# A two-branch sequence kernel: a new written order with finer steps, exchanges issued by SyncE, shared slots and a lead-in of unread products

## The chip, the core and the metric

The kernel runs on one core of a Trainium2 chip. The core has five engines, each with its own queue of instructions that it works through in order: TensorE (PE; its weight loads are listed apart as PEld), VectorE (DVE), ScalarE (ACT), GpSimd (POOL) and SyncE (SP). SP here only issues DMAs, POOL issues DMAs and does a little set-up. Engines wait for each other through semaphores. The metric is the device time of one launch in microseconds; lower is better.

## What is computed

The reference concatenates two results along the last axis, each of 2,048 steps (S) by 1,024 channels (D):

```
A: k_shift = sum over t of k shifted by t steps, times shift_k[:, t]   (4 taps)
   kv = k_shift * v
   y  = irfft(rfft(kv, 2S) * rfft(ssm_k, 2S))[:S] + kv * ssm_D          (long convolution)
   out_a = q * y
B: Lam_bar = exp(dt * Lam), B_bar = ((Lam_bar - 1) / Lam) * B           (complex, 1,024 states)
   h[t] = Lam_bar * h[t-1] + B_bar x[t]
   out_b = 2 * Re(C h) + x * Dskip
```

## The kernel before

**Branch B** takes the sequence in 16 chunks of 128 steps. For chunk i, `x` (L439) loads x transposed. `U` (L444) multiplies it by B on TensorE, into a PSUM bank for every two of the eight groups of 128 states (four calls per chunk, 32 products of 128 columns each); `ue` (L455) copies the bank to SBUF on ScalarE. VectorE then turns the complex recurrence into a real one by a rotation: `r1` (product with the table Z1), `r2` (sum, and from the second chunk the carry), `sc` (two scans of 1,024 elements, and two small instructions that make the next carry), `r3` (product with Z2), `r4` (sum). `y` (L499) multiplies by C on TensorE, `ye` copies, `yst` stores. B and C reach their layout by loads (`bl`, `cl`), transposes on TensorE (`bT`, `cT`) and copies (`bc`, `cc`); eight pieces of C come by transposing DMAs instead (`cx`, L435).

**Branch A** does the convolution as a transform over 4,096 points in two stages, 256 by 16. Stage one: `kvm` and `kva` (L540, L551) make the shifted and weighted k times v on VectorE, `am` multiplies by the constants F1, `ae` copies, `ast` stores to the DRAM tensor Ys_kv. The filter goes the same way: `hl` loads ssm_k, `hT` transposes it, `hc` copies, `hm` multiplies, `he` copies, `hst` stores to Ys_h. Stage two has 32 groups. `lh` and `lk` (L632) load two groups of each tensor at a time in another layout, `lw` (L627) loads the constants W of two groups. For group g: `sh` and `sk` multiply on TensorE (L641), `she` and `ske` copy to SBUF on ScalarE (L651, L660). `sw` (L663) makes a second copy of the filter's result with its upper and lower 64 partitions exchanged, by two DMAs of 128 KB within SBUF. `pr` (L671) multiplies both copies with the other result on VectorE, `sa` (L680) does the inverse stage on TensorE, `sae` copies, `vst` (L693) stores to Vs. Last, `vl` loads Vs in a third layout, `a3` multiplies by G, `a3e` copies, `qm` multiplies by q (loaded by `qp`), `ost` stores.

**What sets the order.** Nothing is scheduled at run time. The string ORDER lists some 1,560 words, such as `U.0.0:p1a6`: the step, its indices, and after the colon the slots of its new tiles. The last loop of the kernel calls the steps in that order, and every engine's queue gets its instructions in the order in which they are called. Two words on different engines are ordered only by the data and by the slots that they share. Slots p0 to p7 are the PSUM banks; b0 to b14 are SBUF tiles of 2 KB per partition; a0 to a10 are tiles of 4 KB (loads of v, q, ssm_k, Vs, and the tiles u, h, hab, vsb); m0 and m1 are VectorE's products; w0 to w2 the constants W. The loads `lh` and `lk` have six slots of their own, h0 to h2 and k0 to k2, in a pool (a2) that takes the place of the one that holds wbc and the ring of k when stage one is done. A new tile in a slot waits until the last reader of the old one is done. DMAs called `spd` (loads, and the transposing ones) go into SP's queue, those called `gpd` (stores, the exchanges, a few constants) into POOL's.

Of the kernel before, what the change touches and what calls it, by code (L numbers as in the profile page):

```python
# [14 lines left out]
ALU = mybir.AluOpType  # L15
F32 = mybir.dt.float32
BF16 = mybir.dt.bfloat16
# [45 lines left out]
CFG = {'kr': 8, 'bdve': 4, 'actsw': ()}  # L63

ORDER = """
ld_par ld_w:a0a1 ld_G bl.2.0:b0 ld_sd bl.0.1:b1 bl.2.1:b2 ld_F x.0:b3 wb.4:p0 bl.3.0:b4 wb.0:p1 bl.7.1:b5 wbe.4 par_T:p2 bl.5.0:b6 wbe.0 bl.5.1:b7
bT.2.0:p3 p32 bl.4.1:b8 exp1 wb.1:p4 bl.0.0:b9 bc.2.0 dve2 bT.0.1:p5 bl.1.0:b10 dve3 wbe.1 sm_pre wb.2:p6 exp2 wb.3:p7 bl.4.0:b11 wbe.2 bT.2.1:p0 dd
wbe.3 cx.7.0 sin0 bT.3.0:p1 bT.7.1:p2 bc.3.0 bl.1.1:b12 wb.5:p3 bl.7.0:b13 bc.0.1 bT.5.0:p4 wbe.5 wb.6:p6 bl.3.1:b14 bc.2.1 bT.5.1:p7 bc.7.1 wb.7:p1
tabA1:a2a3a4a5 cx.6.0 bT.4.1:p5 bc.5.1 bT.0.0:p3 cx.7.1 wbe.6 bT.1.0:p0 bc.4.1 bT.4.0:p2 kp.-2 wbe.7 par_rest bc.0.0 bl.6.0:b0 bc.5.0 x.2:b1 bT.1.1:p7
bc.1.0 bT.7.0:p6 bc.1.1 x.1:b2 tabA2 bT.3.1:p5 bc.7.0 U.0.0:p1a6 hl.0.0:a7 bc.4.0 cl.2.1:b4 bc.3.1 sin2 U.0.1:p3 bl.6.1:b5 ue.0.0 sin1 kp.-1 U.0.2:p4  # L70
ue.0.1 kp.0 eo cl.1.0:b6 bT.6.0:p7 U.2.0:p0a8 hl.0.1:a9 U.1.0:p6a10 cl.2.0:b7 vp.0:a0 ue.2.0 stt U.1.1:p2 cl.1.1:b8 ue.0.2 ue.1.0 bc.6.0 x.3:b9
cT.2.1:p5 ue.1.1 U.1.2:p1 cc.2.1 kp.1 vp.1:a1 z1 cl.0.0:b10 cT.1.0:p3 kvm.0:m0 bT.6.1:p0 U.2.1:p4 cl.3.0:b11 cl.3.1:b12 cc.1.0 kvm.1:m1 U.2.2:p6 z2
kp.2 bc.6.1 cx.4.1 kva.0:b13 cT.1.1:p7 hT.0.0:p2 ue.1.2 vp.2:a2 U.0.3:p5 cc.1.1 ue.2.1 kva.1:b14 cx.5.1 hc.0.0:b0 am.0.0:p3 am.0.1:p0 am.0.2:p1 ue.0.3
am.0.3:p7 U.1.3:p4 cl.0.1:b4 ue.2.2 ae.0.0:b6 cx.4.0 r1.0:m0 ae.0.1 ae.0.2:b5 am.1.0:p2 am.1.1:p5 ast.0.0 ae.0.3 hl.1.0:a3 am.1.2:p6 am.1.3:p3
ae.1.0:b8 cx.5.0 cT.3.0:p0 ast.0.1 ae.1.2:b13 U.2.3:p1 kvm.2:m1 cc.3.0 hl.2.0:a4 ae.1.3 cT.0.0:p7 ae.1.1 ast.1.1 cT.3.1:p2 lw.0:w0 ue.2.3 r2.0:a5
hT.0.1:p6 ast.1.0 cc.0.0 cT.2.0:p0 kva.2:b14 hT.0.2:p3 cc.3.1 hT.0.3:p5 cc.2.0 U.3.0:p1a0 hl.1.1:a6 hc.0.1:b11 sc.0 hc.0.3:b10 am.2.0:p7 am.2.1:p2
am.2.2:p0 am.2.3:p6 ae.2.0:b12 cx.6.1 hm.0.3.0:p5 ae.2.1 hm.0.3.1:p7 ae.2.2:b7 hm.0.3.2:p2 ast.2.0 ae.2.3 x.4:b6 cT.0.1:p0 he.0.3.2:b5 U.3.1:p6
ast.2.1 cc.0.1 he.0.3.0:b14 kvm.3:m0 kp.3 he.0.3.1 U.3.2:p2 ue.3.1 hst.0.3.0 ue.3.0 hc.0.2:b13 r3.0:m1 U.3.3:p0 x.6:b4 ue.3.2 ue.1.3 hm.0.2.0:p5
ue.3.3 hm.0.2.1:p7 hd.0 hm.0.1.0:p6 r4.0 hm.0.3.3:p1 he.0.2.0:b8 hm.0.0.0:p3 x.5:b12 hm.0.0.1:p2 he.0.1.0:b10 hm.0.2.2:p4 hm.0.2.3:p0 he.0.0.0:b7
hm.0.1.1:p5 r1.1:m1 y.0.0.0:p6 he.0.0.1 he.0.1.1 y.0.0.1 hst.0.0.0 he.0.3.3 he.0.2.1 x.7:b13 y.0.0.2 he.0.2.2:b14 r2.1:a7 hst.0.3.1 he.0.2.3 y.0.0.3  # L80
hl.2.1:a9 lw.2:w1 hm.0.0.2:p3 sc.1 hm.0.0.3:p2 hst.0.2.1 hT.1.0:p5 ye.0.0:b0 hT.1.1:p1 lw.1:w2 hm.0.1.2:p7 y.0.1.0:p4 hst.0.2.0 y.0.1.1 hst.0.1.0
he.0.0.2:b7 y.0.1.2 x.9:b3 he.0.0.3 y.0.1.3 r1.2:m1 hm.0.1.3:p0 ye.0.1 hT.1.2:p6 hst.0.0.1 hc.1.0:b11 hT.1.3:p3 U.4.0:p2a10 vp.7:a5 hc.1.3:b5 hd.1
r2.2:a3 yst.0 hc.1.2:b14 hm.1.0.0:p4 hm.1.0.1:p5 sc.2 ue.4.0 vp.3:a6 hm.1.0.2:p3 hm.1.0.3:p6 U.4.1:p2 he.0.1.2:b11 he.0.1.3 he.1.0.0:b8 hst.0.1.1
he.1.0.1 U.4.2:p7 ue.4.1 hst.1.0.0 hc.1.1:b10 U.4.3:p0 ue.4.2 r3.1:m1 he.1.0.2:b7 hm.1.1.0:p4 hm.1.1.1:p5 ue.4.3 hm.1.1.2:p2 hm.1.1.3:p1 he.1.0.3
hm.1.3.0:p7 r4.1 hm.1.3.1:p3 hm.1.3.2:p0 he.1.1.2:b10 hT.2.0:p6 hst.1.0.1 he.1.1.3 hm.1.3.3:p2 kva.3:b0 he.1.1.0:b5 y.1.0.0:p1 he.1.1.1 hst.1.1.1
y.1.0.1 y.1.0.2 he.1.3.2:b11 r3.2:m1 hst.1.1.0 vp.6:a8 he.1.3.3 y.1.0.3 y.1.1.0:p4 hst.1.3.1 ye.1.0:b8 r1.3:m0 y.1.1.1 am.3.0:p5 hc.2.0:b2 am.3.1:p0
am.3.2:p2 am.3.3:p1 r4.2 y.1.1.2 x.8:b0 ae.3.2:b7 ae.3.3 y.1.1.3 r2.3:a1 hl.3.0:a0 ast.3.1 y.2.0.0:p6 ye.1.1 ae.3.0:b10 hd.2 sc.3 y.2.0.1 yst.1 ae.3.1
hm.2.0.0:p2 ast.3.0 hm.2.0.1:p1 hm.2.0.2:p4 hm.2.0.3:p5 y.2.0.2 he.2.0.0:b2 he.2.0.1 y.2.0.3 he.2.0.2:b5 hst.2.0.0 he.2.0.3 y.2.1.0:p0 ye.2.0:b11
y.2.1.1 hst.2.0.1 kvm.4:m1 y.2.1.2 he.1.3.0:b1 he.1.3.1 y.2.1.3 x.10:b7 r3.3:m0 hst.1.3.0 hm.1.2.0:p2 ye.2.1 hm.1.2.1:p1 hm.1.2.2:p4 kp.4 hm.1.2.3:p5
he.1.2.0:b8 hT.2.1:p6 he.1.2.2:b14 yst.2 hT.2.2:p7 he.1.2.3 hT.2.3:p3 kva.4:b10 hc.2.2:b2 hst.1.2.1 U.5.0:p0a7 hl.3.1:a3 hc.2.1:b5 he.1.2.1 r4.3  # L90
U.5.1:p2 ue.5.0 hst.1.2.0 kvm.5:m1 hc.2.3:b1 am.4.0:p4 am.4.1:p5 am.4.2:p7 am.4.3:p6 ue.5.1 y.3.0.0:p1 ae.4.2:b10 kvm.6:m0 ae.4.3 y.3.0.1 ae.4.0:b11
ast.4.1 ae.4.1 y.3.0.2 ast.4.0 y.3.0.3 kp.5 kva.5:b14 y.3.1.0:p0 ye.3.0:b8 y.3.1.1 kva.6:b10 y.3.1.2 vp.4:a4 x.12:b9 am.5.0:p3 am.5.1:p2 am.5.2:p7
ae.5.0:b11 am.5.3:p6 y.3.1.3 ae.5.2:b14 kvm.7:m1 ae.5.3 am.6.0:p4 am.6.1:p5 ye.3.1 am.6.2:p1 am.6.3:p3 ast.5.1 ae.5.1 U.5.2:p7 yst.3 ae.6.0:b10 ae.6.1
ast.5.0 r1.4:m0 ast.6.0 hm.2.1.0:p6 ue.5.2 hm.2.1.1:p0 hm.2.1.2:p2 hm.2.1.3:p4 U.5.3:p5 he.2.1.2:b5 r2.4:a9 he.2.1.3 vp.5:a2 he.2.1.0:b14 hst.2.1.1
he.2.1.1 hm.2.2.0:p7 kva.7:b8 hm.2.2.1:p2 ue.5.3 hm.2.2.2:p4 hm.2.2.3:p6 he.2.2.0:b11 hm.2.3.0:p0 hm.2.3.1:p5 hst.2.1.0 he.2.2.1 hm.2.3.2:p7
he.2.3.0:b2 hm.2.3.3:p2 he.2.3.1 hT.3.0:p0 sc.4 hst.2.2.0 he.2.3.2:b10 am.7.0:p5 he.2.3.3 am.7.1:p7 ae.7.0:b1 am.7.2:p2 hst.2.3.1 ae.7.1 am.7.3:p5
he.2.2.2:b5 hT.3.1:p7 he.2.2.3 hT.3.2:p4 ast.7.0 hc.3.1:b8 U.6.0:p6a1 hst.2.3.0 hc.3.2:b14 kvm.8:m0 ae.6.2:b11 hst.2.2.1 hm.3.2.0:p7 hm.3.2.1:p4
ue.6.0 hm.3.2.2:p1 ae.6.3 hm.3.2.3:p6 he.3.2.2:b10 U.6.1:p3 ast.6.1 he.3.2.3 r3.4:m1 kp.6 he.3.2.0:b14 hst.3.2.1 he.3.2.1 ae.7.2:b1 U.6.2:p1 ae.7.3
hst.3.2.0 ue.6.1 kva.8:b2 hc.3.0:b5 hm.3.1.0:p6 hm.3.1.1:p7 hm.3.1.2:p4 ast.7.1 ue.6.2 hm.3.1.3:p2 hT.3.3:p5 he.3.1.0:b8 U.6.3:p3 he.3.1.1 r4.4
hc.3.3:b11 hst.3.1.0 kvm.9:m0 he.3.1.2:b10 y.4.0.0:p0 he.3.1.3 ue.6.3 am.8.0:p1 hst.3.1.1 am.8.1:p6 ae.8.0:b14 am.8.2:p7 am.8.3:p5 kvm.10:m1 y.4.0.1  # L100
ae.8.1 ae.8.2:b1 ast.8.0 y.4.0.2 ae.8.3 y.4.0.3 ast.8.1 kva.9:b2 kp.7 y.4.1.0:p4 ye.4.0:b8 y.4.1.1 kva.10:b10 am.9.0:p2 x.11:b14 am.9.1:p3 ae.9.0:b6
am.9.2:p1 am.9.3:p6 y.4.1.2 ae.9.1 ae.9.2:b2 y.4.1.3 ast.9.0 ae.9.3 kvm.11:m0 hm.3.3.0:p7 ast.9.1 ye.4.1 am.10.0:p5 am.10.1:p0 am.10.2:p2 ae.10.0:b1
hm.3.3.1:p3 yst.4 hm.3.3.2:p1 ae.10.1 am.10.3:p6 hm.3.3.3:p4 ae.10.2:b10 U.9.0:p5a10 kvm.12:m1 ast.10.0 ae.10.3 he.3.3.2:b11 ast.10.1 he.3.3.3
U.9.1:p0 he.3.3.0:b6 hd.3 hst.3.3.1 ue.9.0 kva.11:b2 he.3.3.1 hm.3.0.0:p2 hst.3.3.0 ue.9.1 hm.3.0.1:p6 hm.3.0.2:p1 hm.3.0.3:p4 he.3.0.0:b8 U.7.0:p7a6
he.3.0.1 kva.12:b1 he.3.0.2:b5 hst.3.0.0 he.3.0.3 am.11.0:p5 ue.7.0 am.11.1:p3 am.11.2:p0 am.11.3:p2 ae.11.0:b10 hst.3.0.1 U.7.1:p6 kvm.13:m0 ae.11.1
ae.11.2:b11 ae.11.3 ast.11.0 U.7.2:p1 ue.7.1 ast.11.1 kvm.14:m1 U.7.3:p4 ue.7.2 kva.13:b2 am.12.0:p7 ue.7.3 am.12.1:p5 am.12.2:p3 am.12.3:p0
ae.12.0:b6 U.8.0:p2a0 ae.12.1 kva.14:b8 ae.12.2:b5 ast.12.0 ae.12.3 am.13.0:p6 ue.8.0 am.13.1:p1 ast.12.1 am.13.2:p4 am.13.3:p7 ae.13.0:b10 U.9.2:p5
r1.5:m0 ae.13.1 ae.13.2:b11 ast.13.0 ae.13.3 am.14.0:p3 ue.9.2 am.14.1:p0 ast.13.1 am.14.2:p2 am.14.3:p6 ae.14.0:b1 kvm.15:m1 U.8.1:p1 ae.14.2:b2
ae.14.1 ae.14.3 ast.14.0 U.8.2:p4 ue.8.1 r2.5:a3 ast.14.1 lh.0:h0 lh.1:h1 lh.2:h2 kva.15:b6 U.8.3:p7 ue.8.2 U.9.3:p5 ue.8.3 sc.5 am.15.0:p3 ue.9.3
am.15.1:p2 am.15.2:p0 sh.0.0:p6 ae.15.0:b8 sh.0.1:p1 sh.1.0:p4 ae.15.1 am.15.3:p7 sh.1.1:p5 ae.15.2:b5 U.11.0:p3a4 lh.4:h0 ast.15.0 ae.15.3 she.0.0:a9  # L110
ast.15.1 she.0.1 r1.6:m0 sh.2.0:p2 she.1.0:a2 sh.2.1:p0 sw.0 sh.4.0:p7 she.1.1 sh.4.1:p6 sh.5.0:p1 she.4.0:a8 sh.5.1:p4 sh.3.0:p5 she.5.0:a7 lh.3:h2
# [55 lines left out]
def full_kernel(ctx, tc, A_q, A_k, A_v, A_shift_k, A_ssm_k, A_ssm_D, B_x, B_Lre, B_Lim, B_Bre, B_Bim,  # L167
# [85 lines left out]
    def k4(name, shape):  # L253
        return rtile(ring, "a", name, shape)
# [115 lines left out]
    def z2():  # L370
        nc.scalar.mul(Z2[:, 2, :, :], Z2[:, 0, :, :], -1.0)
        for n_ in ("vc", "vs", "rn", "ang"):
            st.pop(n_)
# [419 lines left out]
```

## Time and profile before

| what | value |
|---|---|
| runs | 389.32, 392.50, 394.33 us; median 392.5 |
| profiled execution | span 394.4 us from its first to its last instruction; the runs list 394.33 |
| TensorE busy | 366.3 us, 93% of the span |
| VectorE busy | 331.7 us, 84% |
| ScalarE busy | 280.4 us, 71% |
| GpSimd busy, with its DMA issues | 126.9 us, 32% |
| DMA | 101.38 MB, 257 GB/s on average |
| first and last product | 5.14 us; the last ends at 388.9 us |
| mean granted TensorE clock | 0.991 |

Times count from the first instruction of the span. A matmul's listed duration runs until its result has left the array, so that two in a row overlap: 128x512 matmuls are listed with 379 ns but start 216 ns apart. "Idle before" is the time in which an engine had nothing before an instruction, and the name behind the arrow is what ended it. In the chain of waits, each line is a piece of the chain that ended last: its start, its length, and who worked; "issue" is time in which nothing is seen to be waited for. In the list of waits, the numbers are the total in us, how often, and the longest. A granted clock of 0.50 means that TensorE ran at half speed.

### The profile page before, as it was taken

What the parts mean: (1) busy time and instruction counts of PE and PEld (TensorE: products, weight loads), DVE (VectorE), ACT (ScalarE), POOL (GpSimd) and SP (SyncE); (2) the same over time, 40 slices, a digit from 0 to 9 for tenths busy, and PEclk for the clock granted to TensorE, in tenths of its full rate; (3) what the DMA queues carried; (4) which work ended last, traced back from release to release, by engine and by line L of the source; (5) the groups of instructions that cost most, each with busy time, mean ns of one, the idle gap of its engine ahead of it and who ended that gap; (6) DMA issues with size and microseconds to landing.
All of it is one profiled execution on the core that took longest, in us unless ns stands there. A gap on an engine that the chain in (4) does not pass through costs nothing.

```text
span 394.4 us, 8923 instructions
## 1 busy us (share of the span) xinstructions
PE 366.3 (93%) x3529; PEld 246.4 (62%) x3529; DVE 331.7 (84%) x335; ACT 280.4 (71%) x519; POOL 126.9 (32%) x220
## 2 busy tenths in 40 slices
PE   4998998999988999999899699899998989999994
PEld 2898886775737858897366244455546458685441
DVE  4766999899989999999999979889956971999941
ACT  4899997676649969769289559589693994344642
POOL 3000124574716765425213233233240341020142
PEclk9999999999999999999999989999998999999999
DMA  6999999999986767368999997999989868458895
GB/s 192 313 250 290 328 234 280 297 239 373 303 199 225 220 190 249 125 199 295 270 269 296 276 239 244 236 330 268 321 244 284 253 161 295 161 181 285 292 359 216
DMA packets 59076, 101.38 MB, mean 257 GB/s; under 512 B 31102, under 2 KB 33150, under 8 KB 59036
## 3 DMA queue, kind: packets, MB, share of 16 engines
q1 hardware_dynamic: 45308, 58.73, 54.5%
q0 software_dynamic: 13728, 42.10, 33.1%
q8 instruction: 27, 0.44, 0.5%
q14 instruction: 13, 0.11, 0.1%
HBM read 52.57 MB, written 33.55 MB: 218 GB/s over the span
## 4 chain that ended last, share of the span: by engine, by line
PE 23%; issue 19%; DMA 12%; POOL 5%; ACT 3%; DVE 3%; POOLq 0%; SPq 0%; ACTq 0%; DVEq 0%
PE ps_y L506 7%; PE ps_a L641 5%; PE ps_a L680 5%; PE ps_u L453 5%; DMA l2k<-Ys_kv 4%; DMA l2h<-Ys_h 3%; DMA wts<-a_c_W 2%; POOL out_dram L726 2%; DMA hab<-hab 2%; ACT hab L651 1%; POOL Ys_kv L576 1%; DMA Ys_kv<-ysb 1%; DVE mt L546 1%; ACT x L660 1%; PE ps_a L565 0%
## 5 line engine op out<-in xcount | busy, mean ns | idle before, releaser
L506 PE MATMUL ps_y<-CT,h 128*128 128x512 bf16 x512 | 127.2, 381 | 1.3 <-DVE h L495 1.3
L453 PEld LDWEIGHTS <-BT 128*128 128x128 bf16 x2048 | 118.6, 99 | 6.1 <-issue 1.8
L453 PE MATMUL ps_u<-xT,BT 128*128 128x128 bf16 x2048 | 122.0, 220 | 0.4
L506 PEld LDWEIGHTS <-h 128*128 128x128 bf16 x512 | 46.0, 98 | 49.9 <-DVE h L495 2.2
L483 DVE TENSOR_TENSOR_SCAN h<-rtab,h 128x1024 bf16<-128x1024 f32 x32 | 71.5, 2274 | 0.2
L455 ACT CAST u<-ps_u 128x512 bf16<-128x512 f32 x64 | 39.9, 645 | 23.1 <-PE ps_u L453 21.5
L624 POOL DMA_DIRECT2D Ys_h<-ysbh x64 | 46.1, 723 | 23.4 <-ACT ysbh L617 20.6
L671 DVE TENSOR_TENSOR hab<-x,hab 128x2048 bf16<-128x2048 bf16 x32 | 38.8, 1222 | 17.4 <-DMA hab<-hab 11.0
L576 POOL DMA_DIRECT2D Ys_kv<-ysb x32 | 17.5, 549 | 87.2 <-ACT ysb L574 87.0
L465 DVE TENSOR_TENSOR mt<-u,Z 128x4096 bf16<-128x4096 bf16 x16 | 36.6, 2286 | 10.5 <-ACT u L455 10.2
L689 ACT CAST vsb<-ps_a 128x512 bf16<-128x512 f32 x64 | 36.0, 638 | 7.8 <-PE ps_a L680 7.8
L660 ACT CAST x<-ps_a 128x512 bf16<-128x512 f32 x64 | 36.9, 665 | 5.9 <-PE ps_a L641 5.8
L651 ACT CAST hab<-ps_a 128x512 bf16<-128x512 f32 x64 | 35.9, 679 | 7.1 <-PE ps_a L641 7.1
L617 ACT CAST ysbh<-ps_a 128x512 bf16<-128x512 f32 x64 | 34.6, 633 | 8.9 <-DMA Ys_h<-ysbh 5.2
L574 ACT CAST ysb<-ps_a 128x512 bf16<-128x512 f32 x64 | 34.3, 634 | 8.8 <-DMA Ys_kv<-ysb 6.1
L521 ACT CAST yo<-ps_y 128x512 bf16<-128x512 f32 x32 | 19.2, 611 | 26.9 <-PE ps_y L506 25.2
L465 DVE TENSOR_TENSOR mt<-h,Z 128x4096 bf16<-128x4096 bf16 x16 | 36.5, 2284 | 0.0
L680 PE MATMUL ps_a<-hab,wts 128*128 128x512 bf16 x128 | 32.4, 379 | 3.8 <-DVE hab L671 3.5
L546 DVE TENSOR_TENSOR mt<-kring,wbc 128x4096 bf16<-128x4096 bf16 (+3 forms) x16 | 29.9, 1884 | 3.4 <-DMA kring<-in_A_k_dram 3.4
L665 POOL DMA_DIRECT2D hab<-hab x32 | 16.8, 526 | 47.1 <-ACT hab L651 45.0
L511 PE MATMUL ps_y<-Dd,xT 128*128 128x128 bf16 x128 | 28.0, 219 | 0.0
L641 PEld LDWEIGHTS <-wts 128*128 128x128 bf16 x128 | 12.1, 99 | 21.0 <-DMA wts<-a_c_W 3.9
(110 smaller groups left out, 448.0 us busy)
## 6 DMA issues: line engine op xcount, KB each, us to landing
Ys_kv<-ysb POOLq DMA_DIRECT2D x32, 256.0 KB, 3.8
Ys_h<-ysbh POOLq DMA_DIRECT2D x64, 128.0 KB, 4.3
l2h<-Ys_h SPq DMA_DIRECT2D x16, 512.0 KB, 6.7
hab<-hab POOLq DMA_DIRECT2D x64, 128.0 KB, 6.7
l2k<-Ys_kv SPq DMA_DIRECT2D x16, 512.0 KB, 6.6
Vs<-vsb POOLq DMA_DIRECT2D x16, 512.0 KB, 4.9
vv<-Vs SPq DMA_DIRECT2D x32, 256.0 KB, 4.2
hk<-in_A_ssm_k_dram SPq DMA_DIRECT2D x8, 512.0 KB, 8.7
```

What stands on the lines that cost most here:

```text
L453: nc.tensor.matmul(pu[:, w, jl, :], BT[:, 2 * jp + jl, w, d, :], xT[:, d, :], start=(d == 0), stop=(d == ND - 1))
L455: E["ue"] = lambda i, jp: nc.scalar.copy(st["u", i][:, :, 2 * jp:2 * jp + 2, :], st.pop(("pu", i, jp))[:])
L465: nc.vector.tensor_mul(m, s_, win(Z))
L483: nc.vector.tensor_tensor_scan(gf[:, a * W:(a + 1) * W], rt1, gf[:, a * W:(a + 1) * W], 0.0, ALU.mult, ALU.add)
L506: nc.tensor.matmul(py[:], h[:, 1 - w, j, :], CT[:, j, w, dh * 512:(dh + 1) * 512], start=(j == 0 and w == 0), stop=(j == NJ - 1 and w == 1))
L617: nc.scalar.copy(st["yh", qd, n4, w // 2][:, :, w % 2, :], st.pop(("pa", qd, n4, w))[:].rearrange("p (c d) -> p c d", c=2))
L624: gpd(Ys_h[cc, n0:n0 + 2, :, qd * DQ:(qd + 1) * DQ].rearrange("n k d -> k n d"), t_[:, cc, :, :])
L651: nc.scalar.copy(st["hab", g][:, 0, cols], pt[:])
L660: nc.scalar.copy(st["x16", g][:, w * 512:(w + 1) * 512], st.pop(("ps", "l2k", g, w))[:])
L671: nc.vector.tensor_mul(hab[:], st.pop(("x16", g))[:].unsqueeze(1).to_broadcast([P, 2, D]), hab[:])
L680: nc.tensor.matmul(pt[:], st["w", gq][:, gi, 1 + a, :], hab[:, a, w * 512:(w + 1) * 512], start=(a == 0), stop=(a == 1))
L689: nc.scalar.copy(st["vsb", gq][:, gi, w * 512:(w + 1) * 512], st.pop(("ps", "v", g, w))[:])
```

## The change

- `fill.10` stands first in the order: ten products of 512 columns of a tile of zeros into a PSUM bank that nobody reads. The zeros are part of Z1, cleared by VectorE at the very start; Z1 gets its values later.
- Steps are cut finer: `U` by one group of states (128 calls of 16 products), `sc` by one scan, with `rc`, `cm` and `ca` for the three carry instructions, `kva` into `kva`, `kvb`, `kvc`. The instructions stay the same; they can be placed one by one.
- `sw` issues its two DMAs from SP's queue instead of POOL's.
- The slots h0 to h2 and k0 to k2 go, and a11 to a16 come, of the same size and in the same pool: `lh` and `lk` draw on all 17 "a" slots, and so do the other users of them late in the kernel.
- The whole order and all slots are new, 1,723 words. Beside the fill, each step occurs as often as before. Tiles are no longer removed from the table `st` when last read, which changes no instruction; an unused option (`actsw`) goes.

What the order changes where the prediction looks: the first loads on SP are `bl.1.0 bl.2.1 bl.3.1`, then the parameters, six more of `bl`, `cl.2.1` and then `x.0`, with `U.0.1.0` as the first U (in the order before: parameters, `bl.2.0 bl.0.1 bl.2.1 x.0`, with `U.0.0` after thirteen transposed tiles of B). The first `cx` comes after all of B. The first `kvm` is `kvm.3`, ahead of `stt` and `r1.0`. `lk.2` is the first load of Ys_kv.

```diff
-CFG = {'kr': 8, 'bdve': 4, 'actsw': ()}
+CFG = {'kr': 8, 'bdve': 4}
+NA = 11
...
-ld_par ld_w:a0a1 ld_G bl.2.0:b0 ld_sd bl.0.1:b1 bl.2.1:b2 ld_F x.0:b3 wb.4:p0 bl.3.0:b4 wb.0:p1 bl.7.1:b5 wbe.4 par_T:p2 bl.5.0:b6 wbe.0 bl.5.1:b7
...
+fill.10:p7 ld_w:a0a1 wb.1:p0 wbe.1 bl.1.0:b0 bl.2.1:b1 bT.2.1:p1 bl.3.1:b2 ld_par ld_F par_T:p2 p32 bl.0.1:b3 exp1 wb.7:p3 wbe.7 bc.2.1 dve2 wb.4:p4 wb.3:p5
...
+sw.7 pr.7 sk.9.1:p2 sk.9.0:p6 y.6.1.1 sw.6 pr.6 ske.9.0:b5 ske.9.1 y.6.1.2 sa.7.0:p2 y.6.1.3 sa.6.0:p6 sae.6.0:a10 sae.7.0 sw.8 pr.8 sa.6.1:p0 sw.9
...
+    Z1 = wpool.tile([P, 3, NJ, T], BF16, name="Z1")
+    nc.vector.memset(Z1[:, 0, 0:4, :], 0.0)
...
     def k4(name, shape):
-        return rtile(ring, "a", name, shape)
+        if cur["a"][0] < NA:
+            return rtile(ring, "a", name, shape)
+        return rtile(ap_pool("a2"), "a", name, shape)
...
+    def fill(n):
+        pt = ptile("ps_z", [P, 512])
+        z = Z1[:, 0, 0:4, :].rearrange("p j t -> p (j t)")
+        for _ in range(n):
+            nc.tensor.matmul(pt[:], z[:, 0:P], z, start=True, stop=True)
...
-    def U(i, jp):
-        if jp == 0:
+    def U(i, jp, jl):
+        if (jp, jl) == (0, 0):
             st["u", i] = k4("u", [P, 2, NJ, T])
...
     def r2(i):
...
-        if i > 0:
-            nc.vector.tensor_add(g[:, :, :, 0], g[:, :, :, 0], carry[:])
...
+    def rc(i):
+        nc.vector.tensor_add(g[:, :, :, 0], g[:, :, :, 0], carry[:])
...
+    def sc(i, a):
+        gf = st["g", i][:].rearrange("p a j t -> p (a j t)")[:, a * W:(a + 1) * W]
+        nc.vector.tensor_tensor_scan(gf, rt1, gf, 0.0, ALU.mult, ALU.add)
...
     def l2(nm, Ys, gq):
-        st[nm, gq] = rtile(ap_pool("a2"), nm[2], nm, [P, GC, D])
+        st[nm, gq] = k4(nm, [P, GC, D])
...
     def sw(g):
         hab = st["hab", g]
-        gpd(hab[0:64, 1, :], hab[64:128, 0, :])
-        gpd(hab[64:128, 1, :], hab[0:64, 0, :])
+        spd(hab[0:64, 1, :], hab[64:128, 0, :])
+        spd(hab[64:128, 1, :], hab[0:64, 0, :])
```

## The prediction

> **What bounds the kernel now.** I read the page first, then busy time by stage, TensorE's timeline at both ends, the chain of waits, the list of waits and the DMA issues.
>
> ```profile
> span 394.4 us, 8923 instructions
> PE 366.3 (93%) x3529; PEld 246.4 (62%) x3529; DVE 331.7 (84%) x335; ACT 280.4 (71%) x519; POOL 126.9 (32%) x220
> ...
> DMA  6999999999986767368999997999989868458895
> ```
>
> TensorE (PE) is nearly always busy, VectorE (DVE) is second, the DMA engines are full until about 120 us. GpSimd (POOL) is idle two thirds of the time. Busy is not full speed, so I price the products by their spacing, from the chain of waits (start, duration, what):
>
> ```profile
> 155.66 0.87 PE ps_a L609 x8
> ...
> 241.57 0.86 PE ps_a L680 x4
> ...
> 257.17 1.79 PE ps_u L453 x32
> ...
> 287.07 0.63 ACT hab L651
> 287.70 0.28 issue
> 287.98 0.48 POOL hab L665
> 288.51 7.61 DMA hab<-hab
> 296.25 1.24 DVE hab L671
> 297.53 1.04 PE ps_a L680 x4
> ```
>
> That is 0.109, 0.216 and 0.056 us for products of 256, 512 and 128 columns. The program has 128, 904 and 2,497 of them (par_T's small one counted with the last): 14.0 + 195.3 + 139.8 = 349.0 us. The span is 394.4, so 45.4 us are not products: 5.1 before the first product starts, 5.4 after the last ends (388.9), and 34.9 lost in between. Spacing the products of each stage in the same way, the loss falls thus: 7.1 in the first 20 us, 7.3 from 20 to 120, 7.0 from 120 to 200, 13.4 from 200 to 340, none after 340.
>
> ```profile
> 0.00:20.00 20.00, 14.86 (x116) 10.67 (x117) 12.53 (x53) 13.75 (x20) 3.66 (x12) 1.00 0.94 250
> 20.00:40.00 20.00, 18.80 (x334) 18.46 (x332) 13.17 (x24) 20.00 (x37) 0.00 (x0) 1.00 1.07 275
> ...
> 227.00:230.00 3.00, 3.00 (x8) 1.08 (x9) 0.50 (x1) 2.15 (x4) 0.20 (x1) 0.50 0.73 90
> ...
> 340.00:360.00 20.00, 20.00 (x196) 13.23 (x194) 19.83 (x18) 7.72 (x15) 2.71 (x5) 1.00 0.63 201
> ```
>
> Columns: stretch, length, busy time of PE, weight loads, DVE, ACT, POOL, granted clock, DMA share, GB/s. Two things to see. DVE has 25.7 us of work in the first 40, so it starts 14.3 us in arrears and is full afterwards. At 227 the granted clock is 0.50, just after a wait of 2.3 us for l2h; it lasts 3.4 us, comes again at 298.7, and costs 1.6 us each time. The start is as slow, though its clock column says 1.00:
>
> ```profile
> 9.54 2.74 PE L417 MATMUL ps_t<-ident,ld 128*128 128x128 bf16 x24
> ```
>
> 24 products in 2.74 us are 0.11 each, half speed. So it goes from 5.1 to about 18.7 us, 4.3 of the 7.1 us lost there; the other 2.8 are gaps.
>
> ```profile
> DVE hab L671 <- DMA hab<-hab: 11.0, 8, 4.6
> ...
> PEld L641 <- DMA wts<-a_c_W: 3.9, 3, 1.7
> ```
>
> ```profile
> l2h<-Ys_h SPq DMA_DIRECT2D x16, 512.0 KB, 6.7
> hab<-hab POOLq DMA_DIRECT2D x64, 128.0 KB, 6.7
> ```
>
> From 180 to 330 us the loop is: TensorE product (sh), ScalarE copy (she), exchange of the halves of hab by two DMAs (sw), VectorE product (pr), TensorE product (sa). The chain above shows one turn: 9.8 us from the end of the copy to sa.
>
> **How I compare the orders.** I add up each queue's work along the two written orders, with these spacings and the groups' mean durations (DVE's scaled to its 331.7 us). A place in TensorE's queue is so many us of products before it; a cover is the products that lie between a cause and its use. These are sums of rows, not a run of the schedule.
>
> **The change part by part.**
> *Fill.* Ten products of 512 columns at half speed, 0.41 us each (four in 1.87 us at 226.96, less the last one's 0.63), are 4.1 us. They need a small memset on VectorE first (today's of ones ends at 0.99 us), so they run from about 1.2 to 5.3; the first real product starts at 5.14 now. Own cost 0.2. If the clock is then full, 4.3 us of half speed go. But loads then bind: x.0 is now the eleventh large DMA on SP's queue (3.5 us issue today, about 7 then, landing near 13 at the 250 to 300 GB/s of this stage), and U starts at queue place 6.3 instead of 8.1, at 20.3 us today. 13 − 6.3 leaves TensorE 6.7 us late where it is 12.2 late today. ScalarE, saturated from 20 to 60 us, has 38.9 us of copies before r1.0 against 44.6; at its present pace that is r1.0 at 40 instead of 43.8, with more VectorE work (33.0 against 29.4) ahead of it: VectorE's arrears fall from 15 to about 9. TensorE and VectorE gain the same microseconds, so I take one: −4.5. Ends: 0 (loads or ScalarE bind as now) and −7.1.
> The clock rule of the Trainium skill (TensorE: Matmul & The Clock Gate, on the HAM clock gate) says half clock is the default, full clock comes after about 3.4 us of sustained activity, and an idle window of that length takes it away. By it the fill is barely long enough, and a wait for loads at 8 to 13 us undoes it: the start term would shrink to −2. The row agrees on the 3.4 us dips.
> *Finer steps.* U in halves (0.9 us), scans, carries and kv sums apart: same instructions, same work, 0 by themselves. They let the order move: VectorE's work ahead of a TensorE user exceeds TensorE's own by at most 4.3 us instead of 5.4. TensorE waits about 10 us for h and acc today (L506 3.5, L565 7.3): −2.5, ends −6 and +3.
> *First lk.* It waits for all Ys_kv stores. From the last am to the first sk lie 9.4 us of products instead of 14.7; queued behind lk.2 on SP are lk.0, lk.1 and the exchanges 2, 4, 5, 0, 1, for which VectorE waits. Today the last store's landing is 4.7 and the loads take 11 to 14 us in traffic, 5 to 6 at best: +2, ends −1 and +5.
> *Exchanges on SP.* POOL loses 64 issues of 0.52 = 33.6 us, off the path: 0. SP gains 64 of about 0.4 = 26 us in some 130 us where it has 55 other issues: room enough. What counts is landing: 2.2 us at best and 10.4 at worst today, median 6.7, on a queue of their own with the stores. On SP they stand behind l2h, l2k, wts and the x transposes (1.2 to 1.6 us of SP each; x.15 and x.14 stand around exchanges 30 and 25), and behind whatever those wait for. The cover she to sa has a median of 10.8 instead of 11.7; from place 186 on several groups have 7 to 8.5 where they had 11. A turn needs 5 us with a quiet landing, 9.8 as in the chain. The order puts the slow loads early enough that I find most exchanges only 0 to 1 MB behind: −2, for the saved POOL queue (its exchanges stood behind Vs stores, idle 3.0 + 0.9) and VectorE's 11 us of waits; ends −8 and +12 (five groups at 2.4 us).
> The skill's DMA: Bandwidth & Descriptors (Issuing engines are not separate DMA queues) says DMAs of any issuer share the same 16 engines, and another issuer saves issue time alone. By it this term is 0 and the sum 2 us higher; no row here shows an exchange on SP.
> *Six slots.* l2h and l2k no longer have three slots each of their own but share 17: loads can come earlier. TensorE waits 7.7 us for them now (L641: 5.1 and 2.6): −3.5, ends −7.7 and 0. Weights keep three slots, and lw's cover falls from 6.6 to 5.8 us on average, to 4 for lw.6, lw.12 and lw.14, where a load takes 8.0 in the median and 2.5 when quiet: +1.5, ends 0 and +6. Half of the clock dips go with the gaps: −1.5, ends −3.2 and +3.
> *Tail.* vst to first a3 has 17.4 us of products instead of 11.8, but twelve vv reloads (6 MB) must land in the 20 us after; nothing waits there today: 0, ends 0 and +4.
>
> Sum: −4.5 − 2.5 + 2 − 2 − 3.5 + 1.5 − 1.5 + 0 = −10.5. The profiled span, 394.4, lies 1.9 above the median 392.5 (runs 389.32 to 394.33); 394.4 − 10.5 = 383.9 there, **382.0** on the median. A measurement can tell about 2% from no change (384.6 and 400.4).
>
> **Rivals.**
> *The start's gain is given back* (0.25): VectorE and TensorE are locked from 160 to 260 us (lead 4 to 5), and shorter covers return 4 to 8 us. Only the start and one dip stay: 392.5 − 4.5 − 1.5 + 2.5 = 389. For it: the shorter covers of sw, lw, lk. Against: VectorE's smaller arrears carry over.
> *Slower: exchanges behind loads in one queue* (0.13). Two 512 KB loads ahead cost 3.7 us at 280 GB/s; 9.8 + 3.7 against a cover of 8.3 is 5.2 us per group, four groups 21, on −4.5 − 2.5 + 2: 392.5 + 16 = 408. It decides from 1.3 us for each of four groups. Against: SP mostly has its loads out before the copy ends.
> *More than forecast* (0.10): half of the 34.9 lost goes, and the start to 8: 373.
> *The fill does nothing*: the clock falls back while loads bind; the others stay: 392.5 − 8 = 384.5, inside the forecast's range.
>
> **How the numbers follow.** Forecast 0.52 with own range 375 to 388, given back 0.25 (386 to 395), slower 0.13 (395 to 410), more 0.10 (370 to 376). Range: 373 to 399 leaves out some 0.1 above and 0.07 below. Below 384.6 lie three quarters of the forecast and all of the last: 0.39 + 0.10 = 0.49; above 400.4 most of the slower rival, 0.11; between them 0.40.
>
> **What would show it.** Right: products at 0.056 us spacing before 10 us; first U near 13; r1.0 near 40; exchanges landing under 6 us from SP; no l2h wait. Wrong: TensorE waiting for hab over 15 us in all, l2k at the first sk over 4, wts over 8, vv at the end, or more dips to 0.50. If U starts before 14 us and the time does not fall, the given-back rival holds.

## The result and the profile after

The changed kernel takes **405.38 us** (median of four runs, 402.75 to 407.82) against 391.24 for the kernel before on the same chip (four runs, 389.32 to 394.33): a ratio of 1.035, interval [1.0275, 1.0426]. It is slower by 14 us. The forecast was 382.0 with a range of 373 to 399: wrong in its sign.

The profiled execution is the fastest of the four: span 400.9, of a run of 402.75. Set against the 394.4 of before, which was the slowest of its four, the difference is 6.5 us. The two traces explain that part; the rest of the 14 is spread over executions that were not traced, and the experiments below are judged on medians. Now and then a run comes out over 1.5% above the fastest of its kernel; ratios leave such runs out, and so do the medians below. Beside the experiments the kernel before was run again: medians 390.4 to 392.0 us.

From the page of the changed kernel, the lines that answer to the first ones shown of before:

```profile
span 400.9 us, 8807 instructions
PE 363.1 (91%) x3497; PEld 246.4 (61%) x3539; DVE 330.1 (82%) x336; ACT 279.5 (70%) x519; POOL 93.3 (23%) x156
...
DMA  7997969985858867878999797996979985999472
```

The shares of TensorE, VectorE and ScalarE are a point or two smaller (GpSimd's falls to 23% with the exchanges gone), and from 80 to 120 us the DMA row reads 8, 5, 8, 5 where before it read 9, 9, 9, 8. Nothing has become the bound by its work; time is lost in waits. (42 of the 3,539 matmul records are missing, the weight loads are complete.)

The list of waits, with the lines that the forecast had named as signs (total us, times, longest):

```profile
DVE hab L675 <- DMA hab<-hab: 10.8, 7, 3.6
...
ACT hT L608 <- DMA Ys_h<-ysbh: 7.0, 3, 3.4
...
PEld L650 <- DMA wts<-a_c_W: 2.6, 2, 1.7
...
PE ps_a L650 <- DMA l2k<-Ys_kv: 0.7, 1, 0.7
```

None of these bad signs is there: the exchanges are waited for as long as before (11.0), the constants less (3.9), l2h not at all, l2k hardly. What is new is the second line: ScalarE's copy into an `hT` tile waits for a *store* of another tile. The group of these 16 copies shows it whole (busy, mean ns, idle before and what ended it):

```profile
L608 ACT COPY hT<-ps_t 128x1024 bf16<-128x1024 bf16 x16 | 16.5, 1038 | 13.2 <-DMA Ys_h<-ysbh 7.0 <-DMA Ys_kv<-ysb 2.8 <-DMA out_dram<-yo 2.6
```

12.4 us of waiting for three kinds of stores; before, the same group waited 2.0:

```profile
L597 ACT COPY hT<-ps_t 128x1024 bf16<-128x1024 bf16 x16 | 16.6, 1084 | 3.1 <-DMA Ys_h<-ysbh 2.0 <-PE ps_y L511 1.1
```

VectorE's `acc` tiles (from `kvb`), which take b slots too, wait 8.1 us for stores where they waited 1.2. One of ScalarE's waits on the chain of waits, and ScalarE's timeline there:

```profile
60.38 0.60 ACT ysbh L626
61.96 6.46 DMA Ys_h<-ysbh
68.53 1.02 ACT hT L608
```

```profile
64.67 0.70 ACT L472 CAST u<-ps_u 128x512 bf16<-128x512 f32 x1
68.53 1.01 ACT L608 COPY hT<-ps_t 128x1024 bf16<-128x1024 bf16 x1 [3.15 <-DMA Ys_h<-ysbh]
```

The words of the order give the reason: `he.0.2.0:b12` and later `hc.1.0:b12`. The new tile takes the slot of a ysbh tile whose store POOL had just issued, and the store's 6.46 us to landing hold the slot. ScalarE works in order, so everything behind `hc` waits too; TensorE stood still for 3.0 us at 66. Five more such gaps follow, at 88, 90, 98, 105 and 136 us (1.3, 1.4, 0.7, 1.9 and 2.5), each behind an hT, yo or ysbh copy that waits for a store out of its slot. After the last of them the granted clock falls:

```profile
140.00:143.40 3.40, 3.40 (x35) 3.40 (x33) 3.37 (x4) 1.91 (x3) 1.37 (x2) 0.52 0.16 45
```

The Trainium skill (Perfetto Trace Analysis, "DMA Instruction — SWDGE (GPSIMD)") says that the listed end of a DMA issued by GpSimd is when its descriptors are written, not when the data has moved. The trace agrees: the store is listed with 0.7 us on POOL and lands 6.5 us after its issue began, and the slot is held for the second.

**Where the time went.** Lateness is the time at which a product starts, less the sum of the spacings of all products ahead of it in TensorE's queue. Where it stays level, TensorE runs without a loss. Worked out from the traces (queue places in us of products; in the last four columns they hold the fill's 2.2 us):

| place | before | changed | 16 slots | 16, tail, late stores on SP | changed, exchanges on POOL |
|---|---|---|---|---|---|
| 50 | 14.6 | 9.5 | 7.2 | 8.3 | 11.5 |
| 140 | 22.6 | 25.8 | 14.1 | 15.7 | 27.1 |
| 200 | 31.6 | 28.0 | 17.5 | 19.1 | 34.3 |
| 300 | 39.6 | 36.1 | 24.3 | 25.9 | 50.6 |
| 340 | 39.6 | 40.1 | 28.3 | 25.7 | 54.8 |
| last product to end of span | 5.4 | 9.3 | 9.3 | 3.6 | 5.4 |

The change is ahead at place 50, loses 16.3 us to place 140 (t = 60 to 166) where before lost 8.0, wins 6.7 back to place 300, then loses 4.0 in the tail and 3.9 after the last product.

In the tail it is a slot again, on ScalarE's timeline:

```profile
364.39 1.57 ACT L716 CAST ot<-ps_a 128x512 bf16<-128x512 f32 x3
370.75 0.59 ACT L716 CAST ot<-ps_a 128x512 bf16<-128x512 f32 x1 [4.79 <-DMA out_dram<-ot]
```

`a3e.10` takes b10 from `a3e.14`, whose store POOL issued only at 364.7, after its `qm`, and which landed at 370.7. TensorE loses 2.5 us at 368.7, and half clock from 372.2 to 375.6 costs 1.6 more.

### The profile page after: what moved, and what is told of

The parts are those of the page before. It is cut to its first block, busy times and chain, and to the rows that moved or that the text cites. A ratio compares the mean times of both kernels' runs of the same rounds, so it can differ in the third digit from the quotient of the medians.

```text
span 400.9 us, 8807 instructions
## 1 busy us (share of the span) xinstructions
PE 363.1 (91%) x3497; PEld 246.4 (61%) x3539; DVE 330.1 (82%) x336; ACT 279.5 (70%) x519; POOL 93.3 (23%) x156
## 4 chain that ended last, share of the span: by engine, by line
PE 34%; DMA 23%; ACT 15%; issue 14%; DVE 5%; POOL 4%; SPq 1%; DVEq 0%; POOLq 0%; ACTq 0%
PE ps_y L525 11%; PE ps_u L470 9%; DMA Ys_h<-ysbh 7%; DMA hab<-hab 5%; PE ps_a L684 4%; DMA Ys_kv<-ysb 4%; PE ps_a L650 4%; ACT ysbh L626 3%; DMA wts<-a_c_W 3%; POOL Ys_h L633 2%; DVE mt L482 2%; PE ps_t L435 2%; ACT hab L658 2%; ACT ysb L588 2%; DMA out_dram<-ot 1%
## 5 line engine op out<-in xcount | busy, mean ns | idle before, releaser
L470 PEld LDWEIGHTS <-BT 128*128 128x128 bf16 x2048 | 120.6, 99 | 16.0 <-issue 7.5
L470 PE MATMUL ps_u<-xT,BT 128*128 128x128 bf16 x2048 | 126.7, 220 | 2.1 <-ACT u L472 1.2
L675 DVE TENSOR_TENSOR hab<-x,hab 128x2048 bf16<-128x2048 bf16 x32 | 38.3, 1221 | 22.9 <-DMA hab<-hab 10.8
L633 POOL DMA_DIRECT2D Ys_h<-ysbh x64 | 46.2, 725 | 25.9 <-ACT ysbh L626 24.6
L472 ACT CAST u<-ps_u 128x512 bf16<-128x512 f32 x64 | 38.7, 615 | 19.5 <-PE ps_u L470 19.2
L658 ACT CAST hab<-ps_a 128x512 bf16<-128x512 f32 x64 | 37.3, 621 | 9.7 <-PE ps_a L650 9.5
L693 POOL DMA_DIRECT2D Vs<-vsb x16 | 8.5, 536 | 142.0 <-ACT vsb L691 138.5
L588 ACT CAST ysb<-ps_a 128x512 bf16<-128x512 f32 x64 | 35.8, 623 | 5.4 <-PE ps_a L581 3.3
L716 ACT CAST ot<-ps_a 128x512 bf16<-128x512 f32 x32 | 17.1, 600 | 18.6 <-PE ps_a L710 13.7
L620 PE MATMUL ps_a<-hT,F1t 128*128 128x256 bf16 x128 | 20.7, 272 | 6.9 <-ACT hT L608 3.7
```

The lines of the kernel that those rows point to most:

```text
L470: nc.tensor.matmul(pu[:, w, jl, :], BT[:, 2 * jp + jl, w, d, :], xT[:, d, :], start=(d == 0), stop=(d == ND - 1))
L472: E["ue"] = lambda i, jp: nc.scalar.copy(st["u", i][:, :, 2 * jp:2 * jp + 2, :], st["pu", i, jp][:])
L588: nc.scalar.copy(st["ysb", n2, cc][:, dh * 512:(dh + 1) * 512], st["pa", n2, w][:])
L633: gpd(Ys_h[cc, n0:n0 + 2, :, qd * DQ:(qd + 1) * DQ].rearrange("n k d -> k n d"), t_[:, cc, :, :])
L658: nc.scalar.copy(st["hab", g][:, 0, cols], pt[:])
L675: nc.vector.tensor_mul(hab[:], st["x16", g][:].unsqueeze(1).to_broadcast([P, 2, D]), hab[:])
```

## The experiments

The theory: the change is slower because its order, with 15 b slots, makes ScalarE wait for stores out of the slots (stage one and tail), and because its end is longer. Rivals: the exchanges on SP cost the time; the fill costs time or brings none; the new order is bad in itself, whatever the slots.

The finer steps alone needed no run: the old order written in the finer words gives every engine's queue the same instructions in the same sequence as before, plus one small memset. In the trace of the next run TensorE's 3,529 weight loads stand in the sequence of before.

**Old order, exchanges on SP.** The old words, with

```diff
-        gpd(hab[0:64, 1, :], hab[64:128, 0, :])
-        gpd(hab[64:128, 1, :], hab[0:64, 0, :])
+        spd(hab[0:64, 1, :], hab[64:128, 0, :])
+        spd(hab[64:128, 1, :], hab[0:64, 0, :])
```

> The order of before, written with the finer words (each queue then issues the same instructions in the same sequence as before, plus one small memset), no fill; only the exchanges of hab are issued by SyncE. Theory (the loss of the change lies in the new order's slots in stage one and in its tail, not in the exchanges): a little faster than before, 387 to 391 us against 391, exchanges landing in about 5 us instead of 6.7. Rival (the exchanges behind SP's loads are what cost the time): 396 us or more, VectorE waiting over 15 us for hab.

Measured: 396.35 us against 390.43, ratio 1.016 [1.008, 1.025]. The theory's number is missed, the rival's is met, but not for its reason: the exchanges land in 5.3 us and VectorE waits 8.8 us for them, less than before. Two other things got longer. The stretch after the last product is 9.4 us instead of 5.4. And TensorE waits longer for the constants (3.9 before), whose loads now stand behind exchanges in SP's queue (in the trace two of them are issued at 215.3 and 231.0 us, each right behind four exchange DMAs):

```profile
PEld L650 <- DMA wts<-a_c_W: 10.1, 5, 3.9
```

Only the first of the two is shown to cost time: 4.0 of the 6 us are the end. The waits for constants did not make the loop longer than in the trace of before: lateness (as in the table) is 36.1 us at the last product against 39.7.

**The same with the fill.** `fill.10:p7` ahead of the old words.

> The same kernel with the ten products of the zeroed tile ahead of TensorE's queue. Theory: the fill raises the clock of the first transposes, but here x.0 and the loads come as late as before, so little of it is kept: 1 to 4 us less than the run without the fill. Rival (the fill is a cost of 2.2 us and no gain): the same as without it or 2 us more.

Measured: 391.19 us in the profiled run, 397.6 to 398.04 in three others. The traced one gains 5 us over the run above; the others do not show it. Not decided here.

**The change without the fill.**

```diff
-fill.10:p7 ld_w:a0a1 wb.1:p0 wbe.1
+ld_w:a0a1 wb.1:p0 wbe.1
```

> The changed kernel without the ten products. Theory: the time of stage one is set by slots that wait for stores, and it swallows what the start brings: 403 to 408 us, the same as the changed kernel's 405, though the first transposes run at half clock. Rival (the fill costs time): 402 us or less. If the fill's gain were kept to the end: 409 us.

Measured: 408.14 us (404.24 to 408.17), ratio 1.042 [1.031, 1.053]. The rival's 402 is not met: the fill shows no cost. Whether stage one swallows its gain is not told by 408 against 405.

**One more b slot.** The room comes from `ones` (256 bytes per partition), put into a tile that is filled later. The b tiles from 33 to 185 us are dealt to 16 slots, so that as few as possible follow less than 4 us behind the last reader of the tile before, as the trace of the change times them. Order, tail and exchanges stay.

```diff
-    ones = const.tile([1, P], BF16, name="ones")
-    nc.vector.memset(ones[:], 1.0)
+    Z2 = wpool.tile([P, 3, NJ, T], BF16, name="Z2")
+    ones = Z2[0:1, 0, 0, :]
+    nc.vector.memset(ones, 1.0)
...
-he.0.2.0:b12
+he.0.2.0:b8
...
-hc.1.0:b12
+hc.1.0:b4
```

> The changed kernel in the same order, with one more b slot (16 for 15; its room comes from the ones, put into a tile that is free at the start) and the b slots of stage one (33 to 185 us) dealt anew so that hardly any tile waits for a store of the one before it. Tail and exchanges as in the change. Theory: TensorE's gaps behind ScalarE's hT, yo and ysbh at 66, 88, 90, 98, 105 and 136 us (10.8 us, and the 1.6 us clock dip behind the last) go: 393 to 398 us against 405, ScalarE's waits of 10 us for store landings ahead of hT under 3. Rival (the order itself, or traffic, limits stage one): 402 to 406 us, the gaps only change their releaser.

Measured: **391.2 us**, ratio 1.001 [0.997, 1.006] against before: 14 us less than the change, more than expected. The group of hT copies, and ScalarE at the same words as above:

```profile
L608 ACT COPY hT<-ps_t 128x1024 bf16<-128x1024 bf16 x16 | 16.8, 1055 | 1.4 <-DMA Ys_h<-ysbh 0.8 <-PE ps_t L603 0.6
```

```profile
62.38 0.70 ACT L472 CAST u<-ps_u 128x512 bf16<-128x512 f32 x1
62.86 1.14 ACT L608 COPY hT<-ps_t 128x1024 bf16<-128x1024 bf16 x1
```

The copy follows at once. Between places 50 and 140 TensorE loses 6.9 us instead of 16.3. The slots are shown to be the cause of the loss in stage one; order, exchanges and the DMAs themselves are the same. Of the 11.8 us between the two traced spans, 2.3 lie ahead of place 50, where the granted clock differs too (below); 9.4 are stage one. The run changes two things, the number of slots and how they are dealt; the next one parts them.

**The 15 slots dealt anew.** Only the numbers behind the b's change, by the same rule; with 15, `hc.1.0` must still follow `he.0.2.0`.

```diff
-he.0.2.0:b12
+he.0.2.0:b2
...
-hc.1.0:b12
+hc.1.0:b2
...
-hc.3.1:b9
+hc.3.1:b12
```

> The changed kernel with its 15 b slots, those of stage one only dealt anew by the same rule as in the run with 16. Theory (the slots are too few for this order: 13.5 of 15 are held in the mean from 60 to 180 us, so a wait taken from one tile falls to another): 401 to 405 us. Rival (they are enough, only badly dealt): 393 to 398 us as with 16.

Measured: 398.6 us from two runs (396.59 and 400.55), ratio 1.017 [1.008, 1.025]; neither expectation is met. The hT copies still wait 8.3 us for stores:

```profile
L608 ACT COPY hT<-ps_t 128x1024 bf16<-128x1024 bf16 x16 | 16.5, 1036 | 10.4 <-DMA out_dram<-yo 3.2 <-DMA Ys_h<-ysbh 2.8 <-DMA Ys_kv<-ysb 2.3
```

By the medians, dealing anew brings some 7 of the 14 us and the sixteenth slot the other 7. In the traces of stage one the number counts for more: between places 50 and 140 TensorE loses 16.3 us in the change, 13.2 here and 6.9 with 16 slots. So the slots were both too few for this order and badly dealt.

**Exchanges of the change back on POOL.**

```diff
-        spd(hab[0:64, 1, :], hab[64:128, 0, :])
-        spd(hab[64:128, 1, :], hab[0:64, 0, :])
+        gpd(hab[0:64, 1, :], hab[64:128, 0, :])
+        gpd(hab[64:128, 1, :], hab[0:64, 0, :])
```

> The changed kernel with the 64 exchanges of hab issued by GpSimd again, as before. Reading of the traces: the four kernels with the exchanges on SP end 9.3 us after TensorE's last product, the one with them on POOL 5.4, since POOL's closing drain ends 6.9 to 7.0 us after its last store was issued, and 3.2 before. If the exchanges' move is the cause: the end is 5.4 again and the drain 3.2. In the loop the exchanges lie on POOL with the Vs stores: VectorE's waits for hab (10.8 us) stay or grow to 16. Together 400 to 405 us against 405. Rival (SP's queue of loads is what costs the time in the loop): 397 us or less. If the longer drain has another cause: end 9.3 and 405 to 410 us.

Measured: 415.9 us, ratio 1.061 [1.053, 1.069]. The end is 5.4 us, as in before, but the loop loses far more (last column of the table: 23 us from place 140 to 300, 10 in the change). Two lines, of the waits and of the DMA issues:

```profile
DVE hab L675 <- DMA hab<-hab: 20.5, 7, 6.4
```

```profile
hab<-hab POOLq DMA_DIRECT2D x64, 128.0 KB, 4.8
```

So the rival that the exchanges on SP cost the time falls: in this order they save some 10 us, although they make the end 3.9 us longer. The landing is the same as from SP (4.9 in the change), which agrees with the Trainium skill (DMA: Bandwidth & Descriptors, "Issuing engines are not separate DMA queues"): the same 16 engines carry them. That another issuer saves the issue time alone, as the page goes on, does not hold here: 10 us hang on which queue they stand in. How they divide between that queue and the clock dips was not separated (after the first 15 us this trace has 13.6 us at half clock up to the last product, the change 6.8).

**The tail's slots dealt anew,** on top of the 16 slots.

```diff
-a3e.14.0:b15
+a3e.14.0:b0
...
-a3e.10.0:b15
+a3e.10.0:b1
```

> The run with 16 slots, and the slots of the tail (from 330 us) dealt anew too, so that a3e.10 no longer takes the slot whose store was issued just before. Theory: ScalarE's wait of 5.5 us at 353 us goes, with TensorE's gap of 2.7 us and the 1.6 us of half clock that follows it: 387 us against 391; end after the last product still 9.3 us. Rival (the tail is bound by VectorE or by the products): 390 to 392 us.

Measured: 387.74 us, ratio 0.988 [0.982, 0.993]. Lateness no longer grows after place 300 (24.2 to 24.0), and the end is still 9.3 us. As expected.

**The last seven stores on SP,** on top of that.

```diff
-    E["yst"] = lambda i: gpd(out_b[i * T:(i + 1) * T, :], st["yo", i][:])
+    E["yst"] = lambda i: (spd if i in (14, 15) else gpd)(out_b[i * T:(i + 1) * T, :], st["yo", i][:])
...
-    E["ost"] = lambda n2: gpd(oar[:, n2, :], st["ot", n2][:])
+    E["ost"] = lambda n2: (spd if n2 in (5, 8, 7, 4, 0) else gpd)(oar[:, n2, :], st["ot", n2][:])
```

> The same, with the last seven output stores (five of out_a, two of out_b) issued by SyncE instead of GpSimd, so that POOL's last DMA is issued some 8 us earlier. If POOL's closing drain of 7 us is what ends the program: the end after the last product falls from 9.3 to 4 to 5 us, 382 to 384 us in all. Rival (the end is the landing of the last store plus a fixed closing, whoever issues it): 387 us, no change.

Measured: **383.69 us** (381.90 to 385.69), ratio 0.979 [0.973, 0.986]. The end falls to 3.6 us. This version is faster than both kernels, by about 2% against before.

**The same without the fill.**

```diff
-fill.10:p7 ld_w:a0a1 wb.1:p0 wbe.1
+ld_w:a0a1 wb.1:p0 wbe.1
```

> The run with 16 slots, the tail dealt anew and seven late stores on SP (383.7 us), without the ten products of the zeroed tile. Theory: the fill lets the first transposes run at full clock and brings U forward by 4 to 5 us (first U late by 6.4 us with it and 11.2 without it in the two runs of the changed order), and with enough slots nothing swallows that: 387 to 389 us. Rival (the rest of the kernel catches up, the fill is worth nothing at the end): 383 to 385 us.

Measured: 386.12 us, ratio 0.988 [0.980, 0.996], between the two expectations. In the traces lateness at place 50 is 12.8 without and 8.3 with the fill; less the 2.2 us that the fill itself occupies, that is 2.3 us of real gain, and at the end 2.1 us of it are left (30.0 against 25.7). So nothing swallows it, but it is half of the "4 to 5" that was expected, because the fill's own products had been left out of that number. The intervals of the two ratios overlap, so the fill's 2.4 us in the medians are not clear of the noise.

**The old order with everything.** Fill, exchanges and seven late stores on SP (its own last ones), 16 slots dealt by the same rule.

```diff
+fill.10:p7
...
-he.0.2.2:b14
+he.0.2.2:b15
...
-ye.0.0:b0
+ye.0.0:b11
```

> The old order with all that helped the new one: fill, exchanges on SP, 16 b slots dealt anew by the same rule, seven late stores on SP. Theory (with enough slots the new order loses less in stage one and in the loop: 16.9 us of lateness at place 200 against 23.9 in the old order with fill): 387 to 391 us. Rival (the order brings nothing; slots, fill and stores do it all): 381 to 385 us.

Measured: 389.7 us, ratio 0.996 [0.9925, 1.0002]. So with the same helps the new order takes some 6 us less, once it has its slots. This need not be the old order at its best: with its exchanges left on POOL and the other helps it was not run. From place 50 to 140 the old order loses 5.8 us with 16 slots and 6.8 with 15: it hardly needed the sixteenth (one trace of each).

**Two runs on POOL's closing drain,** an instruction at the end of POOL's queue: counted from the end of its last store's issue to the end of the drain. Both stand on the kernel with 16 slots and the tail's slots dealt anew.

```diff
-        spd(hab[0:64, 1, :], hab[64:128, 0, :])
-        spd(hab[64:128, 1, :], hab[0:64, 0, :])
+        (gpd if g < 16 else spd)(hab[0:64, 1, :], hab[64:128, 0, :])
+        (gpd if g < 16 else spd)(hab[64:128, 1, :], hab[0:64, 0, :])
```

> Only to read POOL's closing drain (from its last store's issue to the drain's end: 3.1 us with 213 DMAs issued by POOL, 6.9 to 7.0 with 149): the 16-slot kernel with the exchanges 0 to 15 on POOL and 16 to 31 on SP, so 181 DMAs on POOL. If the drain shrinks with the number issued: about 5 us. If it goes by something else that the exchanges change as a whole: 3.1 or 7.0. The time itself: 390 to 396 us, since half the exchanges lie behind the Vs stores again.

```diff
-    E["yst"] = lambda i: gpd(
+    E["yst"] = lambda i: spd(
```

> The 16-slot kernel with all sixteen stores of out_b on SP: 133 DMAs on POOL, the same stores of out_a. If the drain grows as fewer DMAs are issued: 8 us, less if it counts only the last ones. If it is a fixed 7.0 without the exchanges: 7.0. SP's queue then waits for yo in order, so loads behind it come late: 388 to 396 us.

Measured (one run each): 390.1 and 389.07 us; drains of 2.4 us with 181 DMAs on POOL and 5.8 with 133. Neither a rule of "fewer, longer" nor a fixed value fits. What sets the drain stays open.

## Why the prediction was wrong

By its own terms, as the two profiled executions show them (from the table; the fill's 2.2 us taken off the gain at place 50):

| step | forecast | measured |
|---|---|---|
| start, to place 50 | −4.5 | 9.5 + 2.2 − 14.6 = −2.9 |
| finer steps and their order, 50 to 140 | −2.5 | 16.3 − 8.0 = +8.3 |
| 140 to 300: first lk +2, exchanges −2, six slots −3.5, weights +1.5 | −2 | 10.3 − 17.0 = −6.7 |
| clock dips | −1.5 | two full ones in each, inside the rows above and below |
| tail | 0 | +4.0 |
| after the last product | not priced | 9.3 − 5.4 = +3.9 |
| sum | −10.5 | +6.6 (spans: +6.5) |

- **Start: right in kind, but too large, and what held it up was not what the forecast named.** U starts at 14.9 us (13 forecast), which is 8.6 late at the forecast's place 6.3, without the fill's products (6.7 forecast, 12.2 before); r1.0 starts at 40.1 (near 40). The fill's own cost is 0.4: the first real product starts at 5.58 us against 5.14 (0.2 forecast). Loads do not bind: from its first product on, TensorE's rows have no idle mark up to U.

```profile
10.02 5.05 PE L435 MATMUL ps_t<-ident,ld 128*128 128x128 bf16 x56
14.91 1.28 PE L470 MATMUL ps_u<-xT,BT 128*128 128x128 bf16 x20
```

What held it up is the clock: granted full from 7.0 us, and 0.50 again from 10.4 to 13.8, which costs 1.7 us. By the clock rule that the forecast weighed against the term, a wait for loads would take the full clock away; it went without such a wait, so the −2 worked out that way lies nearer to the −2.9 than the −4.5 does by luck. In the run with 16 slots the clock was full from 4.6 us on, without that dip, and U starts at 13.35. Why it falls back in one execution and not in another stays open.
- **Finer steps: this step failed.** It read the order for VectorE's and TensorE's places alone, "same instructions, same work, 0 by themselves", and bounded the loss at +3. A store holds its slot for 2.2 to 6.7 us from its issue, and the new order is short of slots where the old one was not: in this stretch 16 slots dealt anew save it 9.4 us and the old order 1.0. That it keeps more tiles between copy and store at a time is the likely reason, but no run counts them. The list of waits of before already had ScalarE waiting 15 us for store landings (ysb 6.1, ysbh 5.2, hT 2.0 and smaller ones); no step of the forecast used those lines. In the change they are 20.8 us up to the tail, and 12.4 of them stand ahead of hT, which TensorE, VectorE and the next stores need. The slots' covers were worked out for the exchanges, for lh, lk and lw, not for b. From the list of before:

```profile
ACT ysb L574 <- DMA Ys_kv<-ysb: 6.1, 1, 6.1
...
ACT ysbh L617 <- DMA Ys_h<-ysbh: 5.2, 4, 3.1
```

- **Exchanges on SP: right in sign, for a reason not given.** VectorE's waits for hab stayed as they were (11.0 to 10.8). But with this order and the exchanges on POOL they are 20.5, and the kernel is some 10 us slower. The slower rival, loads ahead of exchanges, did not happen; in the old order the opposite did, constants behind exchanges. No rival of the forecast had the b slots in it.
- **Six slots: right.** No l2h wait is left, 0.7 us of l2k. **Weights:** waits fell to 2.6, not +1.5. **First lk:** 0.8 us of gap, within its range.
- **Dips: wrong.** Two long gaps went, two others came, each with its 3.4 us at half clock. The term also rested on an execution with more dips than most: the traced one has a mean granted clock of 0.991, and of 33 later runs of the same kernel 19 have 0.997 or more.
- **Tail: the forecast's upper end.** It looked at the loads of vv and not at the ot tiles' slots and at the late stores.
- **The end was not looked at.** The forecast counted POOL's relief as "off the path: 0"; POOL's closing drain was on it.

With the slots and the end mended, the same change gives 383.7 us. That the forecast said 382 is luck: in the trace of that version the stretch from 50 to 140 brings 0.6 us (2.5 forecast), the one from 140 to 300 brings 6.8 (2 forecast), and 1.8 come from the end, which was not priced. What it lacked in the change as it stood was 10.8 us in stage one (+8.3 for −2.5) and 7.9 in the tail and after it.

## What to carry to other kernels

When a written order is changed, follow every slot of a tile that is stored: the cover to be compared is from the store's issue to the next copy into that slot, and the price is the DMA's landing in the traffic of that stage, not the listed length of its issue. Waits of a copying engine for stores in the profile of before are the sign that the slots are already tight; a new order that needs more of them at a time can be expected to pay there first. And look at what ends the program after the last product: an engine off the path can be the last one to close.

## What the runs showed of the hardware

- POOL's closing drain ends 3.1 to 3.2 us after its last store's issue ended in the kernels with 213 DMAs on POOL, 6.9 to 7.0 with 149 (in either order), 2.4 with 181, 6.4 and 10.3 with 142, 5.8 with 133, while in before and in the change the last store has landed 1.8 us after the issue. With the last stores issued by SP it lay beside other work. What sets its length is not known.
- In the change a single store of 128 KB (Ys_h) took 2.2 to 6.7 us from issue to landing (3.5 in the median of 64), so a slot's cover has to be sized for the long ones.
- In the change two gaps of 2.5 us on TensorE (at 136 and 368.7 us) were each followed by 3.4 us at half clock, worth another 1.6 us; the longest gap, 3.0 us at 66, was not, and the half clock at 10.4 us followed no listed wait of TensorE at all.
